# First product of the second feed-forward by Strassen's method, both of its weights converted in the first stage

## The chip, the core and the metric

The kernel runs on one NeuronCore of one Trainium2 chip. The metric is the device time of one execution in microseconds (us); the time of the kernel before is the median of three runs. The engines are TensorE (PE: matrix products, with PEld for loading the stationary operand), VectorE (DVE), ScalarE (ACT), GpSimd (POOL) and SyncE (SP), which here issues nearly all DMAs. Each engine works off its own queue in order.

## The reference

```python
scores = x @ state^T / 8;  a = softmax(scores);  xread = a @ state         # per batch and head: 512 x 64, 32 states
scores2 = state @ x^T / 8; a2 = softmax(scores2); sread = a2 @ x
x = concat(xread, sread) -> (8 * 544) x 512 tokens
x = (sigmoid(x @ w_gate) * (x @ w_val)) @ w_out                             # first feed-forward, 512 -> 1536 -> 512
r = maximum(x @ w_in, 0); out = (r * r) @ w_out2                            # second feed-forward, 512 -> 2048 -> 512
```

The weights arrive as float64. The kernel holds every operand of a product as a high and a low part in TensorE's fp32r type and forms each product of tiles with three matmuls (high by high, high by low, low by high): that is `mm3`.

## The kernel before

**Stages.** Tokens are worked in nine blocks: eight of 512 (one per batch, `b` = 0 to 7) and one of 256 with the state tokens of all batches (`b` = 8). The first stage runs 108 units, each one slice `f` of 128 of the 1536 hidden features for one block. `front_x` makes the gate and value products (12 matmuls of 512 columns), the sigmoid (ACT) and their product `g` (DVE); `split_g` splits `g` into `gh` (ACT) and `gl` (DVE); `back1` multiplies by the first `w_out` (12 matmuls) into four PSUM banks `acc0` to `acc3`. Units 0 to 95 are the token blocks; the last twelve (the state stage, `front_s`) are the state block's, with matmuls of 256 columns and weights `ws` that come back from DRAM. Attention, the conversion of the weights and the products of states and weights are laid beside the units by `spread(fns, start, end)`, which gives each step a time in units; `step()` calls what is due. A block's output is stored in `y_dram[b]`.

**The second feed-forward.** `front2(b, f)` multiplies one block by one slice of `w_in` (12 matmuls of 512 columns, four tiles of 128 along the 512 inputs by three), then relu (ACT), square (DVE) and split (ACT, DVE); `back2(b, f, g)` multiplies by a slice of the second `w_out` (12 matmuls) into the four `acc` banks, which collect all 16 slices of a block. So a token block takes 16 x 24 = 384 matmuls of 512 columns, and the state block 192 of 256 and 96 of 512.

**Weights.** `load_raw` fetches 512 KB of float64, and `convert` makes fp32r parts of it: one ScalarE instruction on the low words, five on VectorE (`q`, three `tensor_scalar` on `c`, and the addition `c<-c,q`), then the high part on ScalarE and the low part on VectorE (`busy` is False, so the helper is VectorE).

```python
        nc.scalar.copy(out=w[:, 0, :], in_=cf)
        helper(busy).tensor_sub(out=w[:, 1, :], in0=cf, in1=w[:, 0, :].bitcast(F32))
```

The second feed-forward's 32 tiles are converted by `feed()`: two in the middle of the first stage, four about the state stage, the rest beside the first blocks of the second feed-forward; then all of them stay in SBUF.

**Order.** The instructions are written in the order of the program, and a scheduler then sets each engine's queue by its own estimate of times. Waits are by semaphore: an instruction that waits holds up everything behind it on its engine. Buffers come from pools; a tile of a pool waits until the last reader of the tile whose place it takes is done.

## Time and profile before

| what | value |
|---|---|
| median of three runs | 1541.22 us (1539.25 to 1543.1) |
| the profiled execution | 1542.9 us from its first to its last instruction; its own time is not given apart |
| TensorE busy | 1491.6 us, 97% |
| VectorE, ScalarE, GpSimd busy | 854.6, 724.1, 214.7 us |
| first stage's token blocks and attention | up to about 734 us |
| state stage | about 734 to 789 us |
| second feed-forward | 789 to 1542.9 us |

Matmuls are pipelined: the duration of one (about 390 ns at 512 columns) is longer than the distance at which they follow one another, so a stretch is read by how many matmuls ran in it. The busy share is an average over stages with different limits; a stage is read in its own stretch.

### The profile page before, as it was taken

To read this page: it belongs to the slowest core of one execution; us is meant where nothing else is said; L and a number is where in the kernel's file an instruction comes from. 1 tells how busy PE (TensorE), PEld (TensorE's weight loads), DVE (VectorE), ACT (ScalarE), POOL (GpSimd) and SP (SyncE) were. 2 spreads that over 40 slices of the span, in tenths; PEclk is the share of its full clock that TensorE was granted. 3 is DMA by queue.
4 is the path that set the end of the run, shared out by engine and by line. 5 is a ranking of instruction groups with operands and counts; after the bars stand their busy time and mean duration, and the time that the engine had idled before them with its cause. 6 is when DMAs were issued, how large, how long until landed. Compare 5 with 4: busy or idle time off the path is not lost.

```text
span 1542.9 us, 19143 instructions
## 1 busy us (share of the span) xinstructions
PE 1491.6 (97%) x6744; PEld 1193.9 (77%) x6744; DVE 854.6 (55%) x1550; ACT 724.1 (47%) x1314; POOL 214.7 (14%) x263
## 2 busy tenths in 40 slices
PE   5889999999998999999999999999999999999998
PEld 3558767777776778888898788888888888888887
DVE  7987887778986755555659823323232323323232
ACT  5676765456676867665335522223232222223222
POOL 1123213222332333433000000000000000000000
PEclk8789999999999999999999999999999999999999
DMA  9783888879976433343925300101010000101000
GB/s 280 231 225 97 216 272 284 279 234 256 283 208 172 139 94 110 89 116 108 382 91 152 108 28 4 52 0 55 1 55 0 28 28 0 55 0 42 1 28 15
DMA packets 173105, 185.82 MB, mean 120 GB/s; under 512 B 99536, under 2 KB 108752, under 8 KB 171984
## 3 DMA queue, kind: packets, MB, share of 16 engines
q1 hardware_dynamic: 170736, 183.81, 38.9%
q8 instruction: 53, 0.87, 0.2%
q10 hardware_dynamic: 2272, 0.79, 0.2%
q14 instruction: 44, 0.36, 0.1%
HBM read 120.59 MB, written 63.96 MB: 120 GB/s over the span
## 4 chain that ended last, share of the span: by engine, by line
PE 88%; DVE 6%; DMA 3%; ACT 2%; issue 1%; SPq 0%; DVEq 0%; ACTq 0%
PE acc L192 13%; PE acc L193 13%; PE acc L194 13%; PE psi L194 8%; PE psi L192 8%; PE psi L193 8%; PE ps_g L475 3%; PE psg L192 3%; PE psv L192 3%; PE psg L193 3%; PE psg L194 3%; PE psv L194 3%; PE psv L193 3%; DMA raw<-in_moe_w_out_dram 1%; DMA raw<-in_moe_w_val_dram 1%
## 5 line engine op out<-in xcount | busy, mean ns | idle before, releaser
L200 DVE TENSOR_TENSOR gl<-g,gh 128x512 fp32r<-128x512 f32 (+1 forms) x252 | 179.8, 713 | 235.0 <-ACT gh L199 222.2
L199 ACT CAST gh<-g 128x512 fp32r<-128x512 f32 (+1 forms) x252 | 150.5, 597 | 242.4 <-PE acc L193 212.7
L726 DVE TENSOR_TENSOR g<-r 128x512 f32<-128x512 f32 (+1 forms) x144 | 95.2, 661 | 233.5 <-ACT r L725 233.2
L192 PE MATMUL psi<-xh,wi 128*128 128x512 f32 (+1 forms) x576 | 217.7, 378 | 2.1 <-ACT wi L149 2.1
L194 PE MATMUL psi<-xh,wi 128*128 128x512 f32 (+1 forms) x576 | 217.2, 377 | 0.3 <-DVE wi L150 0.3
L193 PE MATMUL psi<-xl,wi 128*128 128x512 f32 (+1 forms) x576 | 217.3, 377 | 0.0
L192 PE MATMUL acc<-wu,gh 128*128 128x512 f32 x544 | 212.1, 390 | 0.8 <-ACT gh L199 0.8
L193 PE MATMUL acc<-wu,gh 128*128 128x512 f32 x544 | 211.9, 389 | 0.0
L542 POOL TENSOR_TENSOR gg<-gi,gg 128x256 fp32r<-128x256 f32 x192 | 156.4, 833 | 397.1 <-ACT gg L541 396.9
L725 ACT ACTIVATE r<-psi 128x512 f32<-128x512 f32 (+1 forms) x144 | 82.5, 573 | 274.1 <-PE psi L194 274.1
L194 PE MATMUL acc<-wu,gl 128*128 128x512 f32 x544 | 206.3, 389 | 0.0
L193 PE MATMUL acc<-gl,o 128*128 128x512 f32 (+1 forms) x432 | 164.0, 382 | 0.1
L194 PE MATMUL acc<-gh,o 128*128 128x512 f32 (+1 forms) x432 | 162.6, 379 | 0.0
L192 PE MATMUL acc<-gh,o 128*128 128x512 f32 (+1 forms) x432 | 141.9, 384 | 1.4 <-ACT gh L199 1.4
L192 PEld LDWEIGHTS psi<-xh,wi 128*128 128x128 f32 x576 | 108.3, 188 | 24.2 <-ACT wi L149 3.7
L194 PEld LDWEIGHTS psi<-xh,wi 128*128 128x128 f32 x576 | 108.2, 188 | 20.6 <-DVE wi L150 0.7
L193 PEld LDWEIGHTS psi<-xl,wi 128*128 128x128 f32 x576 | 108.4, 188 | 20.3
L192 PEld LDWEIGHTS acc<-wu,gh 128*128 128x128 f32 x544 | 102.1, 188 | 22.4 <-ACT gh L199 1.7
L194 PEld LDWEIGHTS acc<-wu,gl 128*128 128x128 f32 x544 | 102.2, 188 | 21.3
L193 PEld LDWEIGHTS acc<-wu,gh 128*128 128x128 f32 x544 | 102.2, 188 | 20.5
L193 PEld LDWEIGHTS acc<-gl,o 128*128 128x128 f32 x432 | 81.4, 188 | 19.2 <-issue 2.9
L192 PEld LDWEIGHTS acc<-gh,o 128*128 128x128 f32 x432 | 79.0, 189 | 20.6 <-issue 2.4
(122 smaller groups left out, 2422.5 us busy)
## 6 DMA issues: line engine op xcount, KB each, us to landing
gd<-go SPq DMA_DIRECT2D x192, 128.0 KB, 3.4
gi<-gd SPq DMA_DIRECT2D x96, 256.0 KB, 3.6
raw<-in_moe_w_out_dram SPq DMA_DIRECT2D x28, 512.0 KB, 4.4
raw<-in_moe_w_gate_dram SPq DMA_DIRECT2D x48, 256.0 KB, 4.4
raw<-in_moe_w_val_dram SPq DMA_DIRECT2D x48, 256.0 KB, 4.5
wd<-w SPq DMA_DIRECT2D x24, 512.0 KB, 4.1
ws<-wd SPq DMA_DIRECT2D x24, 512.0 KB, 9.5
xn<-in_x_dram SPq DMA_DIRECT2D x32, 256.0 KB, 3.7
```

The lines of the kernel that those rows point to most:

```text
L192: nc.tensor.matmul(ps, lh, rh, start=start, stop=False)
L193: nc.tensor.matmul(ps, lh, rl, start=False, stop=False)
L194: nc.tensor.matmul(ps, ll, rh, start=False, stop=stop)
L199: nc.scalar.copy(out=gh[:, :n], in_=g32[:, :n])
L200: nc.vector.tensor_sub(out=gl[:, :n], in0=g32[:, :n], in1=gh[:, :n].bitcast(F32))
L475: nc.tensor.matmul(ps[j], st_t[rows, l, m, c, :], w[rows, r, :], start=(i == 0), stop=(i == 2))
L542: nc.gpsimd.tensor_sub(out=t[:, 1, g], in0=src, in1=t[:, 0, g].bitcast(F32))
L725: nc.scalar.activation(out=r[:, :n], in_=ps[:, :n], func=AF.Relu)
L726: nc.vector.tensor_mul(out=g32[:, :n], in0=r[:, :n], in1=r[:, :n])
```

## The change

The second feed-forward takes the token blocks in four pairs (`p`) and the hidden features in eight pairs of slices (`q`). For one pair of blocks and one pair of slices the product with `w_in` is a 2 by 2 block product (A11 to A22 of the weights by slice and half of the 512 inputs, B11 to B22 of the tokens by half and block). Before it takes eight block products; now Winograd's form of Strassen's method takes seven, P1 to P7, each of 2 x 3 matmuls of 512 columns. Its sums of weights (S1 to S4) are made once; its sums of tokens (T1 to T4, `x_steps`) once for each pair of blocks, and the seven operands are split into high and low parts (14 tiles each, one copy on ScalarE and one subtraction on VectorE). `front` accumulates P1, P6, P7, P4 in the bank `px`, P5 and P3 in `pz`, P2 in `py`, copies three intermediate states out with ScalarE (`p1`, `p5`, `u`), and joins them to the others with three additions on VectorE; then come square and split of four results. `back` sums two slices in PSUM and adds the result to `y2` in SBUF with VectorE (ScalarE copies the first).

All 32 weight tiles are now converted in the first stage (`prep_steps`, spread from unit 57.2 to unit 94) with sums and two of the low parts on GpSimd; the parts are stored in DRAM (`wi_dram`, `wo_dram`) and read back as needed, 256 KB for each product (`wi`, twelve buffers) and 512 KB for each slice of `w_out` (`wo`, four buffers). The state block is worked in the last pair, by the plain method. The ring of `ws` tiles has eight places instead of ten.

```diff
+    NQ = NF2 // 2
+    wi_dram = {q: dram.tile([P, 8, 2, 256], F32, name=f"wi{q}") for q in range(NQ)}
+    wo_dram = {f: dram.tile([P, 2, 512], F32, name=f"wo{f}") for f in range(NF2)}
...
+        two["prep"] = gen2.enter_context(
+            tc.tile_pool(name="prep", bufs=1, side="right", reuse_waits="tile")
+        )
...
+        jobs = []
+        for q in range(NQ):
+            jobs += [("i", 2 * q), ("i", 2 * q + 1), ("u", 2 * q), ("u", 2 * q + 1)]
...
+        def single(n):
+            cs[n] = to_single(raws.pop(n), False).rearrange("p (s x) -> p s x", s=2)
+
+        def store_u(n):
+            w = two["prep"].tile([P, 2, 512], F32R, tag="w", name="wu")
+            cf = cs.pop(n).rearrange("p s x -> p (s x)")
+            nc.scalar.copy(out=w[:, 0, :], in_=cf)
+            nc.gpsimd.tensor_sub(out=w[:, 1, :], in0=cf, in1=w[:, 0, :].bitcast(F32))
+            nc.sync.dma_start(out=wo_dram[jobs[n][1]], in_=w.bitcast(F32))
+
+        def add(n):
+            a1, a2 = cs[n], cs[n + 1]
+            t = two["prep"].tile([P, 4, 256], F32, tag="s", name="sums")
+            nc.gpsimd.tensor_add(out=t[:, 0], in0=a2[:, 0], in1=a2[:, 1])
+            nc.gpsimd.tensor_sub(out=t[:, 1], in0=t[:, 0], in1=a1[:, 0])
+            nc.gpsimd.tensor_sub(out=t[:, 2], in0=a1[:, 0], in1=a2[:, 0])
+            nc.gpsimd.tensor_sub(out=t[:, 3], in0=a1[:, 1], in1=t[:, 1])
+            sums[n] = t
+
+        def blocks_of(n):
+            w = two["prep"].tile([P, 4, 2, 256], F32R, tag="hl", name="wa")
+            for c, at in ((cs.pop(n), slice(1, 3)), (cs.pop(n + 1), slice(0, 4, 3))):
+                nc.scalar.copy(out=w[:, at, 0], in_=c)
+                nc.vector.tensor_sub(out=w[:, at, 1], in0=c, in1=w[:, at, 0].bitcast(F32))
+            nc.sync.dma_start(out=wi_dram[jobs[n][1] // 2][:, 0:4], in_=w.bitcast(F32))
+
+        def sums_of(n):
+            w = two["prep"].tile([P, 4, 2, 256], F32R, tag="hl", name="ws")
+            t = sums.pop(n)
+            nc.scalar.copy(out=w[:, :, 0], in_=t)
+            nc.vector.tensor_sub(out=w[:, :, 1], in0=t, in1=w[:, :, 0].bitcast(F32))
+            nc.sync.dma_start(out=wi_dram[jobs[n][1] // 2][:, 4:8], in_=w.bitcast(F32))
+
+        steps += [lambda: load(0), lambda: load(1)]
+        for n in range(len(jobs)):
+            steps.append(lambda n=n: single(n))
+            if n + 2 < len(jobs):
+                steps.append(lambda n=n: load(n + 2))
+            if n % 4 == 1:
+                steps += [lambda n=n: add(n - 1), lambda n=n: blocks_of(n - 1), lambda n=n: sums_of(n - 1)]
+            elif n % 4 > 1:
+                steps.append(lambda n=n: store_u(n))
+        return steps
 
...
-            tc.tile_pool(name="gv2", bufs=10, side="right", reuse_waits="tile")
+            tc.tile_pool(name="gv2", bufs=8, side="right", reuse_waits="tile")
...
+    A21, A11, A12, A22, S1, S2, S3, S4 = range(8)
+    PRODUCTS = [("P1", A11), ("P5", S1), ("P6", S2), ("P2", A12), ("P7", S3), ("P3", S4), ("P4", A22)]
...
+        for name, bufs in (("wi", 12), ("wo", 4), ("g2", 18), ("y2", 10), ("t2", 1)):
...
+    def load_wo(q):
+        for f in (2 * q, 2 * q + 1):
+            t = two["wo"].tile([P, 2, 512], F32R, tag="wo", name="wo")
+            nc.sync.dma_start(out=t.bitcast(F32), in_=wo_dram[f])
+            wo[f] = t
+    def load_xin(p, i):
+        half, b = ((0, 0), (0, 1), (1, 1), (1, 0))[i]
+        t = raw_p.tile([P, 2, S], F32, tag="raw", name="xin")
+        nc.sync.dma_start(out=t, in_=y_dram[2 * p + b][:, 2 * half : 2 * half + 2, :])
+        xin[p, half, b] = t
+    def split_x(p, name, k, src):
+        h = two["x"].tile([P, S], F32R, tag="x", name="xh")
+        l = two["x"].tile([P, S], F32R, tag="x", name="xl")
+        nc.scalar.copy(out=h, in_=src)
+        nc.vector.tensor_sub(out=l, in0=src, in1=h.bitcast(F32))
+        xop[p, name, k] = (h, l)
+    def x_steps(p):
+        t1, t2 = {}, {}
+        def one_two(k):
+            b11, b12, b22 = (xin[p, i, j][:, k, :] for i, j in ((0, 0), (0, 1), (1, 1)))
+            split_x(p, "P1", k, b11)
+            t1[k] = cv_p.tile([P, S], F32, tag="c", name="t1")
+            nc.vector.tensor_sub(out=t1[k], in0=b12, in1=b11)
+            split_x(p, "P5", k, t1[k])
+            t2[k] = q_p.tile([P, S], F32, tag="q", name="t2")
+            nc.vector.tensor_sub(out=t2[k], in0=b22, in1=t1.pop(k))
+            split_x(p, "P6", k, t2[k])
+        def rest(k):
+            b12, b22, b21 = (xin[p, i, j][:, k, :] for i, j in ((0, 1), (1, 1), (1, 0)))
+            split_x(p, "P2", k, b21)
+            t3 = cv_p.tile([P, S], F32, tag="c", name="t3")
+            nc.vector.tensor_sub(out=t3, in0=b22, in1=b12)
+            split_x(p, "P7", k, t3)
+            split_x(p, "P3", k, b22)
+            t4 = cv_p.tile([P, S], F32, tag="c", name="t4")
+            nc.vector.tensor_sub(out=t4, in0=b21, in1=t2.pop(k))
+            split_x(p, "P4", k, t4)
+        return [
+            lambda: one_two(0), lambda: one_two(1), lambda: load_xin(p, 3),
+            lambda: rest(0), lambda: rest(1),
+        ]
+    def product(ps, p, q, name, start):
+        w = take_wi((p, q, name, dict(PRODUCTS)[name]))
+        for k in range(2):
+            h, l = xop[p, name, k]
+            mm3(
+                ps, w[:, 0, k, :], w[:, 1, k, :], h, l,
+                start and k == 0, k == 1, not start,
+            )
+    def snap(ps, name):
+        t = two["t2"].tile([P, S], F32, tag=name, name=name)
+        nc.scalar.copy(out=t, in_=ps)
+        return t
+    def squared(key, c, raw=False):
+        if raw:
+            r = g_p.tile([P, S], F32, tag="sg", name="r")
+            nc.scalar.activation(out=r, in_=c, func=AF.Relu)
+            nc.vector.tensor_mul(out=r, in0=r, in1=r)
+            c = r
+        else:
+            nc.vector.scalar_tensor_tensor(
+                out=c, in0=c, scalar=0.0, in1=c, op0=ALU.max, op1=ALU.mult
+            )
+        h = two["g2"].tile([P, S], F32R, tag="g2", name="g2h")
+        l = two["g2"].tile([P, S], F32R, tag="g2", name="g2l")
+        nc.scalar.copy(out=h, in_=c)
+        nc.vector.tensor_sub(out=l, in0=c, in1=h.bitcast(F32))
+        g2[key] = (h, l)
+    def front(p, q):
+        x = mm_p.tile([P, S], F32, tag="mm", name="px")
+        y = at_p.tile([P, S], F32, tag="at", name="py")
+        z = at_p.tile([P, S], F32, tag="at", name="pz")
+        def joined(ps, t):
+            c = g_p.tile([P, S], F32, tag="g32", name="c")
+            nc.vector.tensor_add(out=c, in0=ps, in1=t)
+            return c
+        product(x, p, q, "P1", True)
+        p1 = snap(x, "p1")
+        product(z, p, q, "P5", True)
+        p5 = snap(z, "p5")
+        product(x, p, q, "P6", False)
+        u = snap(x, "u")
+        product(y, p, q, "P2", True)
+        squared((p, 0, 2 * q), joined(y, p1))
+        product(x, p, q, "P7", False)
+        c22 = joined(x, p5)
+        product(z, p, q, "P3", False)
+        squared((p, 1, 2 * q + 1), c22)
+        product(x, p, q, "P4", False)
+        squared((p, 1, 2 * q), joined(z, u))
+        squared((p, 0, 2 * q + 1), x, raw=True)
+    def back(p, b, q, nt):
         for t in range(nt):
             ts = slice(t * P, (t + 1) * P)
+            acc = acc_p.tile([P, S], F32, tag=f"acc{t}", name=f"o{t}")
+            for i in range(2):
+                f = 2 * q + i
+                gh, gl = g2[p, b, f]
+                mm3(acc, gh[:, ts], gl[:, ts], wo[f][:, 0, :], wo[f][:, 1, :], i == 0, i == 1)
+            if q == 0:
+                y = y2[b, t] = two["y2"].tile([P, DM], F32, tag="y2", name="y2")
+                nc.scalar.copy(out=y, in_=acc)
+                continue
+            y = y2[b, t]
+            nc.vector.tensor_add(out=y, in0=acc, in1=y)
+            if q < NQ - 1:
+                continue
+            if b == 2:
                 for i in range(4):
                     r0 = (4 * t + i) * (S + NS) + S
                     (nc.scalar if i % 2 else nc.sync).dma_start(
+                        out=out[r0 : r0 + NS, :], in_=y[NS * i : NS * (i + 1), :]
                     )
             else:
+                r0 = (2 * p + b) * (S + NS) + t * P
+                nc.sync.dma_start(out=out[r0 : r0 + P, :], in_=y)
...
-    def feed():
-
-        if waiting and (len(waiting) > 1 or not plan2):
-            key, raw, ring = waiting.pop(0)
...
+    spread([close_gen2], 57, 57)
+    spread(prep_steps(), 57.2, 94)
+    for i in range(3):
+        spread([lambda i=i: load_xin(0, i)], u_s + 2, u_s + 2)
...
+    load_wo(0)
+    for fn in x_steps(0):
+        fn()
+    last = NP - 1
+    for p in range(NP):
+        for q in range(NQ):
+            front(p, q)
+            if p == last and q == 0:
+                prep_state_x()
+            if p == last:
+                state_front(p, q)
+            if q == NQ - 1 and p < last:
+                for fn in x_steps(p + 1):
+                    fn()
+            if p < last and NQ - 5 < q < NQ - 1:
+                load_xin(p + 1, q - NQ + 4)
+            for r in ([q - 1] if q else []) + ([q] if q == NQ - 1 else []):
+                if (p, r) != (last, NQ - 1):
+                    load_wo((r + 1) % NQ)
+                for b in range(2):
+                    back(p, b, r, NT)
+                if p == last:
+                    back(p, 2, r, NSTATE // P)
```

**What stands in SyncE's queue where the second feed-forward begins.** `ws` are the last weights of the state stage, `yd<-y` the stores of the state block's output, which wait for its last copies out of PSUM. Before:

```order
L578 DMA ws<-wd_0_238 128x1024
L578 DMA ws<-wd_1_239 128x1024
L578 DMA ws<-wd_2_240 128x1024
L578 DMA ws<-wd_3_241 128x1024
L634 DMA yd_270<-y 128x256 x4
L118 DMA raw<-in_moe_w_out_dram 128x1024
L118 DMA raw<-in_moe_w_in_dram 128x4x256
L118 DMA raw<-in_moe_w_out_dram 128x1024
L118 DMA raw<-in_moe_w_in_dram 128x4x256
```

After:

```order
L563 DMA ws<-wd_3_241 128x1024
L619 DMA yd_294<-y 128x256 x4
L742 DMA wo<-wo_270 128x1024
L742 DMA wo<-wo_271 128x1024
L727 DMA wi<-wi_262 128x512 x7
L727 DMA wi<-wi_263 128x512 x5
L742 DMA wo<-wo_272 128x1024
L742 DMA wo<-wo_273 128x1024
L873 DMA xst<-yd_294 128x1024
```

Before, the raw weights stand behind the stores, and the first slices of the second feed-forward are converted already; now the first `wo` and all the first `wi` stand behind the stores.

**What stands in VectorE's queue between two units of the token blocks** (the products `g32` number 70 and 71 of 96). Before, from the one to the other:

```order
L564 TENSOR_TENSOR g32_6061<-psv_6054,sg_6052 128x512
L200 TENSOR_TENSOR gl_6069<-g32_6061,gh_6068 128x512
L419 TENSOR_TENSOR tmp_5847<-ps_sr_5842,tmp_5847 64x256
L420 TENSOR_TENSOR sw_5793<-tmp_5847 64x128
L386 TENSOR_TENSOR et_5904<-ps_e2_5899,et_5904 128x8x64
L366 TENSOR_REDUCE nm_6034<-e2_5992 128x1
L367 TENSOR_SCALAR nm_6034<-nm_6034 128x1
L564 TENSOR_TENSOR g32_6123<-psv_6116,sg_6111 128x512
```

After, the last twelve rows ahead of the second of these (L118 to L134 are the conversion, `ws` is the low part of the weight sums):

```order
L134 ISA c_6634<-c_6634,q_6635 128x1024
L359 RECIPROCAL sum_6005<-sum_6005 128x1
L118 TENSOR_SCALAR c_6711<-raw_6522 128x512
L130 TENSOR_SCALAR q_6791<-raw_6670 128x512
L122 TENSOR_SCALAR c_6711<-c_6711 128x512
L126 TENSOR_SCALAR c_6711<-c_6711 128x512
L134 ISA c_6711<-c_6711,q_6712 128x1024
L118 TENSOR_SCALAR c_6790<-raw_6670 128x512
L130 TENSOR_SCALAR q_6849<-raw_6749 128x512
L676 TENSOR_TENSOR ws_6610<-sums_6548,ws_6610 128x4x256
L122 TENSOR_SCALAR c_6790<-c_6790 128x512
L549 TENSOR_TENSOR g32_6331<-psv_6324,sg_6315 128x512
```

Before, six instructions stand between the two products, all of attention or of the unit; now 21 do, and 14 of them belong to the conversion.

## Rows read from the trace of the kernel before

**Rows 1.** The page's head, busy times of the engines, chain that ended last

```profile
span 1542.9 us, 19143 instructions
...
PE 1491.6 (97%) x6744; PEld 1193.9 (77%) x6744; DVE 854.6 (55%) x1550; ACT 724.1 (47%) x1314; POOL 214.7 (14%) x263
...
PE 88%; DVE 6%; DMA 3%; ACT 2%; issue 1%; SPq 0%; DVEq 0%; ACTq 0%
```

**Rows 2.** Busy us (instructions) per engine by stretch, granted clock, DMA share, GB/s

```profile
200.00:440.00 240.00, 238.28 (x977) 170.27 (x976) 199.03 (x351) 144.68 (x266) 63.27 (x80) 1.00 0.86 267
439.90:680.80 240.90, 231.44 (x1061) 188.06 (x1060) 150.72 (x285) 172.37 (x325) 90.73 (x101) 0.98 0.46 127
...
800.00:820.00 20.00, 20.00 (x90) 16.57 (x89) 19.72 (x44) 11.53 (x19) 0.00 (x0) 1.00 0.49 161
900.00:1400.00 500.00, 500.00 (x2208) 414.01 (x2207) 149.04 (x217) 131.02 (x218) 0.00 (x0) 1.00 0.06 22
```

**Rows 3.** Lines by form, TensorE, 900 to 1400 us: busy us, mean ns

```profile
L192 PE MATMUL psi<-xh,wi 128*128 128x512 f32 x368 | 143.2, 389 | 0.0
```

**Rows 4.** The page's costliest groups, TensorE: busy us, mean ns, idle before, releaser

```profile
L192 PE MATMUL psi<-xh,wi 128*128 128x512 f32 (+1 forms) x576 | 217.7, 378 | 2.1 <-ACT wi L149 2.1
```

**Rows 5.** Lines by form, VectorE, 200 to 500 us: a weight conversion's six instructions

```profile
L146 DVE CUSTOM_DVE_ANT_0 c<-c,q 128x1024 uint16<-128x1024 uint16 x33 | 24.1, 733 | 0.5
L150 DVE TENSOR_TENSOR w<-c,w 128x512 fp32r<-128x512 f32 x28 | 20.1, 717 | 2.4 <-ACT w L149 2.4
L134 DVE TENSOR_SCALAR c<-c 128x512 f32<-128x512 f32 x33 | 19.1, 582 | 0.4
L138 DVE TENSOR_SCALAR c<-c 128x512 uint32<-128x512 uint32 x33 | 17.3, 527 | 0.3
L142 DVE TENSOR_SCALAR q<-raw 128x512 uint16<-128x512 uint16 x33 | 17.1, 518 | 5.1 <-DMA raw<-in_moe_w_val_dram 4.8
L130 DVE TENSOR_SCALAR c<-raw 128x512 uint32<-128x512 uint32 x33 | 16.2, 493 | 0.3
```

**Rows 6.** Lines by form, VectorE, 500 to 720 us

```profile
L200 DVE TENSOR_TENSOR gl<-g,gh 128x512 fp32r<-128x512 f32 x36 | 34.4, 955 | 17.7 <-ACT gh L199 17.4
L564 DVE TENSOR_TENSOR g<-psv,sg 128x512 f32<-128x512 f32 x35 | 24.0, 686 | 24.2 <-ACT sg L558 10.5 <-PE psv L194 8.5 <-PE ps_so L429 4.9
```

**Rows 7.** Lines by form, VectorE, 900 to 1400 us

```profile
L200 DVE TENSOR_TENSOR gl<-g,gh 128x512 fp32r<-128x512 f32 x92 | 63.7, 692 | 157.2 <-ACT gh L199 146.6 <-PE psi L193 10.6
```

**Rows 8.** Lines of the whole span: ScalarE's and GpSimd's forms

```profile
L542 POOL TENSOR_TENSOR gg<-gi,gg 128x256 fp32r<-128x256 f32 x192 | 156.4, 833 | 397.1 <-ACT gg L541 396.9
...
L128 ACT ACTIVATE q<-raw 128x512 uint16<-128x512 uint32 x92 | 72.9, 794 | 41.7 <-DVE c L146 26.3 <-DMA raw<-in_moe_w_val_dram 6.5 <-issue 4.9
...
L149 ACT CAST w<-c 128x512 fp32r<-128x512 f32 x48 | 29.8, 620 | 16.3 <-DVE c L146 8.5 <-PE ps_g L475 5.7 <-issue 1.6
```

**Rows 9.** Timeline, TensorE, end of the state stage: start, us, instruction

```profile
789.24 0.28 PE L194 MATMUL acc<-gh,o 128*128 128x256 f32 x1
789.36 0.40 PE L192 MATMUL psi<-xh,wi 128*128 128x512 f32 x1
```

**Rows 10.** Timeline, SyncE's queue: start and us of the issues

```profile
794.49 1.78 SPq L634 DMA_DIRECT2D yd<-y  x4
```

**Rows 11.** DMA issues: count, KB each, median us to landing

```profile
gi<-gd SPq DMA_DIRECT2D x96, 256.0 KB, 3.6
...
raw<-in_moe_w_in_dram SPq DMA_DIRECT2D x16, 512.0 KB, 4.8
```

**Rows 12.** Stretches of 2 us after TensorE had stood (columns as in rows 2)

```profile
494.00:496.00 2.00, 0.87 (x4) 0.58 (x3) 0.32 (x2) 0.92 (x5) 0.34 (x1) 0.50 1.08 336
...
498.00:500.00 2.00, 2.00 (x9) 1.70 (x8) 0.87 (x2) 1.51 (x5) 0.72 (x1) 0.50 0.55 143
500.00:502.00 2.00, 2.00 (x11) 1.65 (x10) 1.47 (x3) 1.95 (x6) 0.85 (x1) 0.99 0.47 131
```

**Rows 13.** Lines of the whole span: VectorE's squaring in the second feed-forward

```profile
L726 DVE TENSOR_TENSOR g<-r 128x512 f32<-128x512 f32 (+1 forms) x144 | 95.2, 661 | 233.5 <-ACT r L725 233.2
```

More of the change, by code (lines that the diff above doesn't have):

```diff
@@ L119, in load_raw, with to_single @@
         return raw
[L121 removed]
+    def to_single(raw, busy):
         lo, hi = raw[:, :, 0], raw[:, :, 1]
@@ L148, in convert @@
         )
+        return cf
+    def convert(raw, w, busy):
+        cf = to_single(raw, busy)
         nc.scalar.copy(out=w[:, 0, :], in_=cf)
@@ L731, in back2 @@
-    def back2(b, f, g):
-        nt = width(b) // P
-        if f == 0:
-            accs[b] = new_acc()
-        acc = accs[b]
-        gh, gl = g
-        w = need(("u", f))
+        for name, bufs in (("wi", 12), ("wo", 4), ("g2", 18), ("y2", 10), ("t2", 1)):
+            two[name] = ctx.enter_context(
+                tc.tile_pool(name=name, bufs=bufs, side="right", reuse_waits="tile")
+            )
+    NP = B // 2
+    wi, wo, xin, xop, g2, y2 = {}, {}, {}, {}, {}, {}
+    wi_plan = []
+    for p in range(NP):
+        for q in range(NQ):
+            wi_plan += [(p, q, name, at) for name, at in PRODUCTS]
+            if p == NP - 1:
+                wi_plan += [(p, q, "s", at) for at in (A11, A12, A21, A22)]
@@ new lines, with feed_wi, take_wi @@
+    wi_done = [0, 0]
+    def feed_wi(n):
+        while wi_done[0] < min(wi_done[1] + n, len(wi_plan)):
+            p, q, name, at = key = wi_plan[wi_done[0]]
+            t = two["wi"].tile([P, 2, 2, P], F32R, tag="wi", name="wi")
+            nc.sync.dma_start(
+                out=t.bitcast(F32), in_=wi_dram[q][:, at].rearrange("p l (k f) -> p l k f", k=2)
+            )
+            wi[key] = t
+            wi_done[0] += 1
+    def take_wi(key):
+        feed_wi(11)
+        assert wi_plan[wi_done[1]] == key
+        wi_done[1] += 1
+        return wi.pop(key)
@@ L857 @@
         held.append(lambda b=b, f=f, lo=lo, hi=hi, g=g: back1(b, f, lo, hi, g))
-        if b == B and f == 2:
-            prefetch(0)
-    for _ in range(NA):
-        feed()
     drain(0)
```

159 lines of the change are left out of this document (52 added, 107 removed).

## Prediction

> **What bounds the kernel now.** I read the page's head first: of a span of 1542.9 us TensorE is busy for 97%, and the chain that ended last lies on it for 88% [rows 1]. A busy share is a mean over stages, so I next took the stretches [rows 2]. In the second feed-forward, from 900 to 1400 us, TensorE has no gap, the granted clock is 1.00, the upper of its two levels, and VectorE and ScalarE are busy for under a third of it. The reader is to see that 2208 matmuls went through in 500 us, one per 500 / 2208 = 0.2264 us; the 0.389 us that the lines give for one matmul [rows 3] is its duration with the overlap in it and would overstate any saving. Here only fewer matmuls help, or a wait that is taken away. Between 439.9 and 680.8 us, where the conversion is put, TensorE is the fullest as well (231.4 of 240.9 us), but VectorE works for 150.7, ScalarE for 172.4 and GpSimd for 90.7 [rows 2]: idle are 90.2, 68.5 and 150.2 us. That is the room the conversion has.
>
> The sum is made against the profiled execution, whose span is 1542.9 us; the median of the runs lies 1.7 us lower, and I take that off at the end.
>
> **Fewer matmuls.** For a pair of blocks and a pair of slices there are 7 products of 6 matmuls in place of 8: 4 pairs x 8 pairs of slices x 6 = 192 matmuls of 512 columns go. The products with the second `w_out` keep their number, and so does the state block. 192 x 0.2264 = **-43.5 us**. The feed of converted weights beside the first blocks goes too, and with it the waits of `psi` for the high part: **-2.1** [rows 4].
>
> **The conversion in the first stage.** On VectorE a tile takes three operations on `c`, one `q` and one addition: 0.582 + 0.527 + 0.493 + 0.518 + 0.733 = 2.853 us [rows 5]. With 32 tiles that is 91.3 us. For the low parts come 16 instructions of 0.717 [rows 5], 11.5 us, and 8 of twice that size, put at 1.43, 11.5 us: in all 184 instructions and 114.3 us. Two conversions stood in this stretch before: 2 x 3.57 = 7.1 us go. So 107 us are to go into 90 us of idle VectorE: 17 too many. The queues are in order, and a product `g` waits behind the conversion instructions that stand before it (14 of the 21 in the piece of order shown), so not every gap is filled; I add 5 for that: **+22 us**. The nearest whole stretch, 200 to 440 us, had VectorE busy for 199 of 240 us at TensorE's side with no visible delay [rows 2]; here it is to be busy all the time. The bounds: if the durations overlap as in 800 to 820 us, where 44 instructions, most of them of conversions, filled 19.72 us [rows 2], one per 0.448, the 184 take 82 us and fit: 0. TensorE's own order is unchanged in this stage, so I see no gain below that. Upward: `gl`, of the same form as the low part, took 0.692 us where GpSimd had no work [rows 7] and 0.955 in 500 to 720 us beside it [rows 6]; the low part stands at 0.717 in rows 5. If all of the 114.3 us stretched by 0.955 / 0.717 = 1.33, it would be 152, and less 7 and 90, 55 too many. I stay at 22, since the rows of 5 come from a stretch that has GpSimd's work beside it too.
>
> That same comparison is where a rule speaks against this change. The Trainium skill (SBUF — State Buffer, Who interferes with whom) says that VectorE's second pair of ports is shared with GpSimd under an exclusive lock, so that of two such instructions one waits out the other. By that rule `gl`, with two inputs in SBUF, should stretch and `g`, with one in PSUM, should not, and the trace agrees: `g` stays at 0.686 us beside GpSimd [rows 6], `gl` does not. By the rule alone the stage would cost the upper bound, which is the third rival's.
>
> ScalarE gets 32 x 0.794 for `q` [rows 8], 32 high parts of 0.620 [rows 8] and eight of double size among them more, about 50 us of its 68.5; GpSimd 32 sums of 128x256 at 0.833 [rows 8] and 16 low parts of twice the size at about 1.67: 53 us of its 150. Both fit, though ScalarE barely, and each high part stands between two VectorE instructions. The DMAs grow most: 30 more raw tiles, 16 parts of `w_out` of 512 KB and 16 of `w_in` sums and blocks of 1 MB are about 40 MB in this stretch, beside the 31 that its mean of 127 GB/s makes: some 295 GB/s. From 200 to 440 us, with as many conversions, 267 GB/s filled 0.86 of the DMA engines and TensorE worked on [rows 2], so I count no time of its own; but loads land later, and SyncE's queue holds all of them in order behind stores that wait for low parts. That is part of what the upper bound stands for.
>
> **The state stage.** Loads of `xin` stand among the `ws` loads in SyncE's queue, splits of tokens stand in VectorE's and ScalarE's ahead of state products, and `ws` has eight places in place of ten. A load of 512 KB lands in 4.8 us [rows 11]. One such landing exposed, or a bit more, is the upper bound, 8 us; the lower is 0; I take **+3**, half of one landing and a little.
>
> **Where the second feed-forward begins.** Before, `psi` follows the last `acc` shown within 0.12 us [rows 9], and other products of the state stage are laid beside it. After, the first `wo` and `wi` stand in SyncE's queue behind four stores of `yd`, and these wait for the state stage's last copies out of PSUM (0.6 us by the nearest copy [rows 8]). So TensorE waits for the copy, four issues of 1.78 us together [rows 10], the issues of two `wo` (0.45 each, by the same row), a landing of 3.6 us for 256 KB [rows 11] and part of the 1 MB of `wo` ahead: about 7.3 us. After standing, the clock is 0.50, the lower level, and is at 0.99 only in the third stretch of 2 us after work resumed [rows 12]; 4 to 5 us at half pace lose 2.2. **+9.5**, between 5 (the `wi` pass the `wo` on other DMA queues, and no fall of the clock) and 14 (both `wo` land whole before it).
>
> **The turns between pairs.** At each of three turns the tokens of the next pair are added and split: 14 splits and 8 sums on VectorE, together with the last results of the old pair some 40 instructions of 0.69 us or 27.6, beside the last round's 111 matmuls, 25.1 us. Short by 2.5 us at each, less if it begins earlier: between 0 and 7.5, **+5**.
>
> **The rounds between.** A round has 90 matmuls, 20.4 us. VectorE has 3 joins and eight additions into `y2`, each with one input in PSUM, as `g` has at 0.686 [rows 6], three squarings by an instruction that has no row (nearest: 0.661 [rows 13]), one more squaring, and four low parts of 0.692 [rows 7]: 19 instructions, 13 us or 64%. ScalarE has less. The waits that are new (P6 waits for the copy of P1 out of its bank, P7 for that of P6, P4 for the join) have five or more microseconds of other products between them in TensorE's order. So 0; the cover is gone if VectorE runs a few microseconds late, which is the last rival's price. Weights read back are 2.8 MB a round, 140 GB/s, below the 161 that a stretch has shown [rows 2].
>
> Sum: -43.5 - 2.1 + 22 + 3 + 9.5 + 5 = -6.1, so 1536.8, and less 1.7 **1535 us**.
>
> **The rivals.** (1) The conversion is nearly hidden: VectorE's gaps take it, as the pitch of 0.448 us allows, and the stage costs 8, the state stage 1, the start 7, the turns 0.5. -45.6 + 16.5 = -29.1: **1512 us**. For it speaks that TensorE's order in the first stage is the same and a unit has slack ahead of it; against, that ScalarE and VectorE hand each tile to and fro five times in order. (2) VectorE becomes the bound of the first stage, slowed by GpSimd, whose work rises from 90.7 to about 144 us in that stretch: the products `g`, and the loads behind the stores that wait for VectorE, come late, and TensorE waits in each unit. The stage costs 45, nearer to the bound of 55 than to the forecast's 22, and the rest is as forecast: -45.6 + 62.5 = +16.9, **1558 us**, slower. It decides from 28 us on, where the sum is zero. For it speaks 0.955 against 0.692; against, that the rows of 5 include some of that. (3) The change saves matmuls but TensorE waits in each round, for the squaring without a row, or for a join, about 1 us in each of 32 rounds: +32, **1567 us**. For it speaks only that this instruction isn't in the trace; against, 36% of VectorE's time to spare.
>
> **How the numbers follow.** The forecast has 0.42, with its own range from 1522 (stage at its middle, others low) to 1547; rival 1 has 0.26, rival 2 0.24, rival 3 0.08. No change, within 0.3% (about what a measurement of this kernel can tell), is 1536.6 to 1545.8. Faster: rival 1 and a little over half of the forecast's, 0.49. Same: 0.17. Slower: rivals 2 and 3 and a sliver, 0.34. The range runs from 1508, a little below rival 1, to 1562, a little above rival 2.
>
> **What would show it.** In the profile after: in a stretch of steady rounds as long as 900 to 1400 us about 2208 matmuls still; fewer would mean rival 3, with TensorE idle by `px` or `pz` released by VectorE or ScalarE. The last token unit of the first stage at about 734 + 22 us, with TensorE's idle time named after `gl` or `gh`; at 742 it is rival 1, at 779 rival 2, and then `w`, `wa` and `ws` take 1.2 times their 0.717 per 512 elements or more. TensorE idle for 7 us ahead of the first `px`, released by the `wi` load, and the clock at 0.50 behind it. The prediction is wrong if the matmuls of the rounds don't stand 0.2264 us apart, or if the conversion delays the first stage by something other than VectorE.

## The result, and the profile after

| | median of the runs | profiled execution's span | TensorE busy | granted clock, mean |
|---|---|---|---|---|
| before | 1542.01 us (4 runs) | 1542.9 us | 1491.6 us | 0.982 |
| changed | 1555.61 us (4 runs) | 1554.3 us | 1470.6 us | 0.971 |

The ratio is 1.0085, 95% interval 1.0071 to 1.0100: slower by 13.6 us. The forecast was 1535 and faster; the time lies inside its range of 1508 to 1562, on the side that had a chance of 0.34.

The page's head after, against [rows 1]: TensorE is busy for 21 us less and yet the span is 11 us longer, VectorE has 250 us more.

```profile
span 1554.3 us, 19917 instructions
...
PE 1470.6 (95%) x6552; PEld 1169.8 (75%) x6552; DVE 1104.3 (71%) x1897; ACT 739.8 (48%) x1343; POOL 280.5 (18%) x311
...
PE 80%; DVE 7%; DMA 4%; ACT 4%; issue 3%; POOL 2%; SPq 0%; ACTq 0%; POOLq 0%; DVEq 0%
```

To see where the time went, cut both spans at the same work: at the start of the 58th of VectorE's 108 products `g` (the conversion has begun), of the 94th (its steps end by there), of the 97th (the first of the state block) and of the 108th (the last). Counted from one like this, they belong to the units 57, 93, 96 and 107. Busy times by stretch, columns as in rows 2; before:

```profile
481.44:716.59 235.15, 225.69 (x1052) 186.12 (x1051) 131.68 (x257) 163.77 (x314) 90.11 (x99) 0.98 0.40 112
716.59:741.86 25.27, 22.20 (x114) 18.33 (x113) 19.58 (x37) 13.67 (x28) 2.76 (x3) 1.00 0.61 236
741.86:788.19 46.33, 45.97 (x380) 45.42 (x379) 17.74 (x44) 13.17 (x29) 0.00 (x0) 1.00 0.70 257
```

After, the same three stretches and 500 us of steady rounds:

```profile
481.10:763.03 281.93, 242.98 (x1040) 190.31 (x1040) 237.17 (x423) 197.38 (x372) 153.75 (x145) 0.93 0.73 233
763.03:794.15 31.12, 25.60 (x128) 21.91 (x126) 18.03 (x36) 18.45 (x35) 5.36 (x5) 0.89 0.59 203
794.15:839.62 45.47, 45.00 (x375) 45.00 (x376) 16.96 (x36) 11.29 (x27) 0.00 (x0) 1.00 0.60 221
900.00:1400.00 500.00, 500.00 (x2241) 415.46 (x2240) 316.04 (x497) 152.72 (x265) 0.00 (x0) 1.00 0.49 167
```

The conversion's stretch lasts 281.9 us in place of 235.2, 46.8 more. Subtract TensorE's busy time from the length: it stood for 39.0 us instead of 9.5, and was "busy" for 243.0 instead of 225.7 with the same matmuls. Of this second part, 17.3 us, the clock makes about 11: read in stretches of 0.5 us, TensorE was busy at the lower level, 0.50, for 30.1 us instead of 8.4, and half of that is lost. The other 6 us are busy time at the upper level that these rows don't divide further. The next stretch costs 5.9 more, the state block 0.9 less. From the last `g` to the end (788.19 to 1542.9, 839.62 to 1554.3) it is 714.7 us instead of 754.7: the second feed-forward gives back 40.0, and 51.8 - 0.3 (the 58th product began that much earlier) - 40.0 is the 11.4 by which the spans differ (rounded by 0.1).

What TensorE waited for in the conversion's stretch (total, times, longest, us):

```profile
PE psg L186 <- ACT sg L543: 20.7, 10, 6.0
PE acc L186 <- ACT gh L193: 3.2, 4, 1.5
PE ps_sr L396 <- POOL xs L385: 2.6, 2, 2.3
PE acc L187 <- DVE gl L194: 2.4, 4, 1.5
```

The sigmoid `sg` frees the bank of PSUM for a later `psg`. It came up to 6 us late, and the timeline shows what stood before it in the longest case. ScalarE, up to the longest wait (start, us, idle before it in brackets):

```profile
655.61 0.18 ACT L424 COPY xs_t<-ps_so 64x32 f32<-64x32 f32 x1 [3.09 <-DVE xs_t L426]
658.34 0.62 ACT L652 CAST wu<-c 128x512 fp32r<-128x512 f32 x1 [2.55 <-DVE c L134]
658.87 0.77 ACT L116 ACTIVATE q<-raw 128x512 uint16<-128x512 uint32 x1
659.66 1.28 ACT L357 ACT_TABLE_LOAD   x1
...
662.57 1.28 ACT L543 ACT_TABLE_LOAD   x1
663.86 0.60 ACT L543 ACTIVATE sg<-psg 128x512 f32<-128x512 f32 x1
```

VectorE in the same microseconds:

```profile
652.72 0.95 DVE L118 TENSOR_SCALAR c<-raw 128x512 uint32<-128x512 uint32 x1 [0.64 <-POOL sums L661]
653.59 1.77 DVE L194 TENSOR_TENSOR gl<-g,gh 128x512 fp32r<-128x512 f32 x1
655.40 0.18 DVE L426 COPY xs_t<-ps_so 64x32 f32<-64x32 f32 x1
655.61 0.63 DVE L122 TENSOR_SCALAR c<-c 128x512 f32<-128x512 f32 x1
656.27 0.85 DVE L126 TENSOR_SCALAR c<-c 128x512 uint32<-128x512 uint32 x1
657.16 1.11 DVE L134 CUSTOM_DVE_ANT_0 c<-c,q 128x1024 uint16<-128x1024 uint16 x1
```

And TensorE:

```profile
664.51 0.80 PE L186 MATMUL psg<-a,gg 128*128 128x512 f32 x1 [6.04 <-ACT sg L543]
```

VectorE waits for GpSimd's sums before it may write `c`; then `gl` takes 1.77 us; a copy of attention that ScalarE waits for comes after it; then ScalarE's next instruction, the high part `wu`, waits for the end of the conversion of `c`; only behind that come the exponential of attention and the sigmoid, with an `ACT_TABLE_LOAD` of 1.28 us before each. Two stretches of these microseconds (columns as in rows 2):

```profile
654.00:660.00 6.00, 4.17 (x19) 2.85 (x18) 5.83 (x9) 1.82 (x4) 4.68 (x5) 1.00 0.55 176
660.00:665.00 5.00, 0.49 (x1) 0.49 (x2) 3.62 (x11) 4.96 (x9) 2.09 (x3) 0.74 0.96 320
```

First VectorE is nearly full (5.83 of 6.00 us) and ScalarE waits for it, then ScalarE is (4.96 of 5.00) with what has gathered behind the wait.

### The profile page after: what moved, and what is told of

The parts are those of the page before. It is cut to its first block, busy times and chain, and to the rows that moved or that the text cites. A ratio compares the mean times of both kernels' runs of the same rounds, so it can differ in the third digit from the quotient of the medians.

```text
span 1554.3 us, 19917 instructions
## 1 busy us (share of the span) xinstructions
PE 1470.6 (95%) x6552; PEld 1169.8 (75%) x6552; DVE 1104.3 (71%) x1897; ACT 739.8 (48%) x1343; POOL 280.5 (18%) x311
## 4 chain that ended last, share of the span: by engine, by line
PE 80%; DVE 7%; DMA 4%; ACT 4%; issue 3%; POOL 2%; SPq 0%; ACTq 0%; POOLq 0%; DVEq 0%
PE o L187 8%; PE o L188 8%; PE o L186 8%; PE acc L187 5%; PE acc L186 5%; PE acc L188 4%; PE px L186 4%; PE px L187 4%; PE px L188 4%; PE ps_g L463 4%; PE psg L186 3%; PE psv L186 3%; PE psg L187 3%; PE psg L188 3%; PE psv L187 2%
## 5 line engine op out<-in xcount | busy, mean ns | idle before, releaser
L858 DVE TENSOR_TENSOR y<-o,y 128x512 f32<-128x512 f32 x238 | 161.9, 686 | 81.1 <-PE o L188 79.9
L187 PE MATMUL o<-wo,g2h 128*128 128x512 f32 x544 | 211.7, 389 | 0.0
L186 PE MATMUL o<-wo,g2h 128*128 128x512 f32 x544 | 211.6, 389 | 0.0
L188 PE MATMUL o<-wo,g2l 128*128 128x512 f32 x544 | 210.3, 389 | 0.0
L188 PEld LDWEIGHTS o<-wo,g2l 128*128 128x128 f32 x544 | 102.1, 188 | 21.2
L187 PEld LDWEIGHTS o<-wo,g2h 128*128 128x128 f32 x544 | 102.1, 188 | 21.1
L186 PEld LDWEIGHTS o<-wo,g2h 128*128 128x128 f32 x544 | 102.1, 188 | 20.9
L186 PE MATMUL px<-xh,wi 128*128 128x512 f32 x256 | 99.5, 392 | 7.7 <-DMA wi<-wi 7.7
L187 PE MATMUL px<-xl,wi 128*128 128x512 f32 x256 | 100.2, 391 | 0.0
L186 PEld LDWEIGHTS acc<-gh,o 128*128 128x128 f32 x432 | 80.0, 190 | 26.3 <-ACT gh L193 5.5
L188 PE MATMUL px<-xh,wi 128*128 128x512 f32 x256 | 99.2, 391 | 0.0
L194 DVE TENSOR_TENSOR gl<-g,gh 128x512 fp32r<-128x512 f32 (+1 forms) x108 | 83.8, 775 | 20.5 <-ACT gh L193 20.4
L463 PE MATMUL ps_g<-w,st_t 64*128 64x512 f32 x288 | 84.5, 475 | 11.5 <-ACT w L141 5.4
L188 PEld LDWEIGHTS acc<-gh,o 128*128 128x128 f32 x432 | 82.8, 192 | 15.5 <-issue 0.7
```

The lines of the kernel that those rows point to most:

```text
L186: nc.tensor.matmul(ps, lh, rh, start=start, stop=False, skip_group_check=more)
L187: nc.tensor.matmul(ps, lh, rl, start=False, stop=False, skip_group_check=more)
L188: nc.tensor.matmul(ps, ll, rh, start=False, stop=stop, skip_group_check=more)
L194: nc.vector.tensor_sub(out=gl[:, :n], in0=g32[:, :n], in1=gh[:, :n].bitcast(F32))
L463: nc.tensor.matmul(ps[j], st_t[rows, l, m, c, :], w[rows, r, :], start=(i == 0), stop=(i == 2))
L858: nc.vector.tensor_add(out=y, in0=acc, in1=y)
```

## Experiments

Three theories for the 46.8 us: V, VectorE is full there; D, the transfers; H, hand-offs in in-order queues. Each run's ratio is against the kernel before as timed beside it: 1544.83 us for the first four runs, 1543.84 for the next three and the first of the runs with late pairs, 1545.31 for "High parts on VectorE" and four late pairs, 1544.19 for "VectorE alone" and five late pairs.

**One pair converted** (1508.78 us, ratio 0.9772, 0.9757 to 0.9786): seven of eight pairs of slices are left out, and the steps of the one are spread up to unit 61.8 instead of 94.

```diff
-        for q in range(NQ):
+        for q in range(1):
             jobs += [("i", 2 * q), ("i", 2 * q + 1), ("u", 2 * q), ("u", 2 * q + 1)]
```

> Leaves out the conversion of seven of the eight pairs of slices (loads, arithmetic and stores); every product reads the parts of the first pair. Theories for the 46 us that the first stage lost between products 58 and 94: V, VectorE is full there and its operations are lengthened by GpSimd's; D, the added transfers (some 40 MB) hold up the loads that the units need; H, the conversion hands each tile to and fro between VectorE, ScalarE and GpSimd, and the units wait behind it in in-order queues. All three give 1505 to 1515 us here (1555.6 less seven eighths of 46 to 52). If the loss came from the other edits of that stage (the pools that close at unit 57), the time would stay above 1535.

So the conversion is what costs: its seven pairs make 47 us of the time (50 when each kernel is set against the runs of before beside it), and with a single pair the rest of the change gains 36.

**Transfers alone** (1532.22 us, 0.9928, 0.9912 to 0.9945).

```diff
+            if n > 3:
+                copy_out(n)      # the raw tile to DRAM: 2 x 512 KB for w_in, 512 KB for w_out
+                return
```

> As the run with one pair converted, but the raw tiles of all 32 are loaded, and stored again to DRAM in the bytes and the number of the parts (1 MB for each tile of w_in, 512 KB for each of w_out); the arithmetic of the other seven pairs is left out. V and H: within 8 us of the run with one pair. D: within 10 us of the changed kernel, so over 1545.

Neither: 23.4 us above one pair. With no arithmetic to hold them back the transfers come in a burst, and TensorE is slowed in it. In the first 62 us it stands for 8.2 us more than with one pair (numbers in the last section); the rest of the loss comes up to about 720 us, at DMA shares of 0.50 to 0.98. The first 62 us (columns as in rows 2; DMA share next to last):

```profile
478.00:500.00 22.00, 12.05 (x50) 8.21 (x48) 11.09 (x21) 10.52 (x19) 7.36 (x8) 0.77 0.99 259
500.00:520.00 20.00, 16.39 (x73) 12.77 (x74) 17.85 (x34) 16.02 (x31) 10.56 (x9) 1.00 1.03 386
520.00:540.00 20.00, 16.05 (x66) 12.45 (x65) 14.03 (x26) 11.38 (x21) 4.72 (x5) 0.85 1.01 325
```

**Arithmetic alone** (1552.40 us, 1.0057, 1.0039 to 1.0075).

```diff
-            cs[n] = to_single(raws.pop(n), False)...
+            cs[n] = to_single(raws.pop(n) if n < 2 else raws[2 + n % 2], False)...
+            if n < 4:      # ahead of each store and of the loads
```

> The arithmetic of all 32 tiles stays (the tiles after the fourth are made from the third and fourth raw tile again), but 28 raw loads and all stores but those of the first pair are left out; every product reads the first pair's parts. V and H: at least 30 us above the run with one pair, 1540 to 1553. D: within 10 us of the run with one pair.

43.6 us above one pair, without 28 loads and most of the stores. D falls as the cause in the changed kernel: the arithmetic alone makes nearly all of the loss, and the two costs don't add (23 + 44 against 47).

**Nothing of the conversion on GpSimd** (1564.07 us, 1.0134, 1.0118 to 1.0149).

```diff
-            nc.gpsimd.tensor_sub(out=w[:, 1, :], in0=cf, in1=w[:, 0, :].bitcast(F32))
+            nc.vector.tensor_sub(out=w[:, 1, :], in0=cf, in1=w[:, 0, :].bitcast(F32))
```

(and the four sums likewise)

> The sums of weights and the low parts of w_out on VectorE in place of GpSimd: 48 instructions more on VectorE, 16 x 0.69 + 32 x 0.36 = 22.6 us, and 54 us less on GpSimd. If VectorE's work alone counts, 15 to 23 us slower, about 1575. V with GpSimd's share in it: the shorter operations give about as much back, 1545 to 1560. H: the waits for GpSimd's results go (30 us of GpSimd's and VectorE's idle time stand against them in the trace), 1535 to 1545.

By the ratios (1.0134 against 1.0085, intervals apart) 0.5% or 7.6 us slower than the changed kernel: above H's band, a little above that of V with GpSimd's share, and well below the 1575 of VectorE's work alone. Saving the waits for GpSimd did not pay for 15 us more of VectorE's busy time.

**One VectorE operation fewer in each conversion** (1550.81 us, 1.0043, 1.0027 to 1.0060).

```diff
-            nc.vector.tensor_scalar(out=c, in0=hi, scalar1=1, scalar2=1, op0=ALU.logical_shift_left, ...)
-            nc.vector.tensor_scalar(out=cf, in0=cf, ... op0=ALU.max, op1=ALU.min)
+            nc.vector.tensor_scalar(out=cf, in0=hi.bitcast(F32), ... op0=ALU.max, op1=ALU.min)
```

> Leaves out the first of the five VectorE operations of each of the 32 conversions (the one that takes the sign off; negative weights come out wrong): 32 instructions of 0.63 us, 20 us less on VectorE, everything else in place. V (VectorE's work is what is short): 15 to 20 us below the changed kernel, about 1537. H (the gaps in the in-order queues, not the work): at most 5 us below it, 1550 to 1556. The run that put 22.6 us more on VectorE lost only some 6, which speaks for H.

Nearer H's number than V's: 6.5 us by the ratios. VectorE's busy time fell by 14.8 us (table below) and not by 20, so each microsecond brought 0.44.

**Five pairs converted** (1536.35 us, 0.9951, 0.9936 to 0.9965): `range(5)` in place of `range(NQ)`.

> Converts five of the eight pairs of slices, spread over the same units; the products of the last three pairs read the parts of the first three. VectorE then has about 66 us more than before in a stretch where it had 103 idle. V as an overflow: at most 10 us above the run with one pair, 1509 to 1519. H, a cost for each tile that is handed about: four sevenths of the 47 us between one pair and eight, about 1535.

V as an overflow of the stretch as a whole falls: VectorE was busy for 198 of 265 us, a quarter of it idle, and still the run is 28 us above one pair (28.6 against the runs of before beside each). Between one, five and eight pairs the cost is a straight line, 7 us a pair.

But the run did not thin the conversion out, as it was meant to. The conversion's last instruction on VectorE started at 633 us with five pairs and at 726 with eight, which from 481 on is 30 to 31 us a pair in both. While it ran, VectorE was nearly as full as in the changed kernel, and behind it TensorE had few gaps. Five pairs, then the changed kernel:

```profile
520.00:560.00 40.00, 35.03 (x156) 27.04 (x157) 37.92 (x67) 29.81 (x58) 25.54 (x24) 1.00 0.73 244
560.00:600.00 40.00, 32.20 (x136) 24.75 (x135) 37.71 (x68) 30.67 (x55) 21.37 (x20) 0.93 0.68 223
640.00:680.00 40.00, 37.03 (x174) 30.32 (x173) 22.39 (x43) 26.88 (x53) 17.07 (x19) 1.00 0.37 101
...
520.00:560.00 40.00, 34.63 (x147) 27.00 (x148) 38.18 (x66) 29.09 (x58) 23.13 (x23) 0.96 0.69 241
560.00:600.00 40.00, 33.20 (x144) 25.50 (x142) 37.08 (x65) 29.92 (x53) 22.47 (x21) 0.96 0.67 215
640.00:680.00 40.00, 32.18 (x138) 25.31 (x138) 32.94 (x61) 26.62 (x50) 23.59 (x24) 0.91 0.77 247
```

So a VectorE that is nearly full for as long as the conversion runs would give the same straight line, and this run does not rule it out.

**The state block's stores on ScalarE's queue** (1551.63 us, 1.0051, 1.0036 to 1.0066).

```diff
-            nc.sync.dma_start(out=to[:, e, :], in_=y[:, :n])
+            (nc.scalar if b == B else nc.sync).dma_start(out=to[:, e, :], in_=y[:, :n])
```

> The four stores of the state block's output go out on ScalarE's queue, so the first loads of wo and wi no longer stand behind them on SyncE's. If TensorE's 7.7 us there are the stores and their wait, 2 to 5 us come back: 1550 to 1554. If the loads wait for the buffers, which the last state products release, no change.

About 5 us back, 0.34%. The one wait of 7.7 us ahead of the first `px` (below) becomes three of 0.9, 2.0 and 0.9: the stores ahead of the loads were half of it, the loads' own landing the rest.

**High parts on VectorE** (1572.87 us, 1.0181, 1.0166 to 1.0196). The stall shown above suggested to take ScalarE out of the conversion.

```diff
-            nc.scalar.copy(out=w[:, 0, :], in_=cf)
+            nc.vector.tensor_copy(w[:, 0, :], cf)
```

> The high parts of the conversion (16 for w_out, 16 and 8 of double size for w_in) are made on VectorE instead of ScalarE: 40 copies, some 24 us, more on VectorE. Theory H in its sharper form, from the trace of the changed kernel around 655 to 664 us: the sigmoid stands on ScalarE behind a copy that waits for c of the conversion, and TensorE waits for the sigmoid. Without these copies ScalarE has nothing of the conversion that waits for VectorE: the 21 us of TensorE's waits for the sigmoid mostly go, and the time is 1535 to 1548. If it is VectorE's work: 6 (by the slope of the run without GpSimd) to 24 us slower, 1562 to 1580.

My sharper theory falls. TensorE's waits up to the 94th product, to be held against the list of the changed kernel:

```profile
PE psg L186 <- ACT sg L543: 11.1, 9, 2.0
PE psv L186 <- DVE g L549: 9.7, 10, 2.2
PE acc L187 <- DVE gl L194: 7.4, 10, 1.7
```

The wait for the sigmoid is halved, as expected, and waits for VectorE's own `g` and `gl` take its place; the backlog shows behind the 94th product, where the stretch up to the 97th takes 49.5 us instead of 31.1.

**VectorE alone** (1533.95 us, 0.9933, 0.9918 to 0.9948).

```diff
+            nc.vector.tensor_scalar(out=c, in0=raws[2 + n % 2][:, :, 1], ...)
+            for _ in range(4):
+                nc.vector.tensor_scalar(out=cf, in0=cf, scalar1=LOW_END, scalar2=HIGH_END, ...)
+            # and 28 tensor_sub in all; nobody reads them
```

> One pair of slices is converted as in the changed kernel; for the other 28 tiles only VectorE works, for as long as it would: five tensor_scalar instructions for each and 28 subtractions between them, without loads, stores, ScalarE or GpSimd and with results that nobody reads (all products read the first pair's parts). Occupancy (the units' own instructions stand behind the conversion's on VectorE, whatever hands it on): 30 to 45 us above the run with one pair, 1540 to 1553. Hand-offs (the waits between VectorE, ScalarE and GpSimd cost, not VectorE's time): at most 15 us above it, under 1524.

Between the two: 25.8 us above one pair (0.6 is taken off one pair's time for the runs of before beside it). So more than half of the 43.6 that the whole arithmetic costs is there when VectorE's instructions are handed to no other engine, and with less of them than meant: VectorE has 79 us more than with one pair, the whole arithmetic 102 (table below). The rest comes with the missing work, the hand-offs and the longer instructions (`c<-c,q`, 0.856 us with GpSimd's part of the conversion beside it, [rows 5] 0.733); these runs don't part the three.

The runs whose work on VectorE differs, from the 58th product to the 97th:

| run | VectorE busy, us | length, us | TensorE standing, us |
|---|---|---|---|
| before | 151.3 | 260.4 | 12.5 |
| one pair | 157.3 | 267.2 | 15.9 |
| three pairs (below) | 183.4 | 281.1 | 25.5 |
| four pairs (below) | 198.3 | 286.2 | 28.4 |
| five pairs | 213.1 | 292.5 | 33.7 |
| VectorE alone | 236.4 | 293.5 | 30.2 |
| one operation fewer | 240.4 | 309.9 | 45.3 |
| changed kernel | 255.2 | 313.1 | 44.5 |
| arithmetic alone | 259.3 | 310.3 | 44.4 |
| without GpSimd | 270.3 | 323.2 | 55.2 |
| high parts on VectorE | 280.8 | 331.2 | 65.3 |

From one pair to eight VectorE's 97.9 us more make the stretch 45.9 longer, 0.47 us for each; from one to five 25.3 for 55.8, 0.45. The run with VectorE alone lies below this line: 26.4 for 79, 0.33.

**Part of the conversion beside the second feed-forward.** There VectorE is busy for 316 of 500 us in the changed kernel's steady rounds, so the last pairs go there (with a ring of six `wi`).

```diff
-    spread(prep_steps(), 57.2, 94)
+    spread(prep_steps(0, 5), 57.2, 94)
+    late = prep_steps(5, NQ)          # a slice of it behind each front(0, q)
```

> Five pairs of slices are converted in the first stage, the last three beside the first four rounds of the second feed-forward, where VectorE has a third of its time idle and GpSimd nothing to do; the ring of wi has six places instead of twelve to make room. V: the first stage costs some 10 us, the rounds 0 to 5 more: 1515 to 1525. H: the first stage still costs about 29, 1537 to 1545.

1538.27 us (0.9962, 0.9947 to 0.9976), 2 above the run that leaves three pairs out: by the rounds they are nearly free. V's number fails and H's holds. With four late, the stores on ScalarE's queue and the next pair's tokens loaded in one round:

> Four pairs of slices converted in the first stage, four beside the first six rounds of the second feed-forward, the state block's stores on ScalarE's queue, the next pair's tokens loaded in the last round but one. By the straight line between one, five and eight pairs (6.7 us each) the first stage gives back 7 us against five pairs, the stores some 4: 1525 to 1531. If four late pairs don't fit beside the rounds (VectorE there has 7 us idle in each of 20.4), TensorE waits for wi and it is 1535 or more.

1527.48 us (0.9887, 0.9871 to 0.9904), as the line says. With five:

> As the run with four pairs late, but five are late, beside the first six rounds. By the straight line the first stage gives back another 7 us: 1520 to 1523. If VectorE's idle third of the rounds can't hold five pairs (about 60 us of it in six rounds against 115 instructions of 0.5 to 0.7 us, 58 to 80), TensorE waits for wi in the rounds 3 to 7 and the time is 1527 or more.

1521.51 us (0.9845, 0.9829 to 0.9862): some 23 us faster than the kernel before, and still converting three pairs beside the units. Its waits of TensorE for `wi` in the second feed-forward are 1.9, 1.8 and 1.7 us, all before 830 us. Behind them its trace shows no wait of TensorE, though VectorE was all but full while the late pairs were converted:

```profile
850.00:950.00 100.00, 100.00 (x443) 82.81 (x442) 97.78 (x168) 44.27 (x71) 22.03 (x20) 1.00 0.91 323
```

## Why the prediction was wrong

**The step that failed is the conversion in the first stage, +22 forecast and 46.8 measured.** The prediction had it in two parts. The first, "17 too many", was the overflow of 107 us into 90 idle ones. Between the 58th and the 94th product VectorE has 237.2 - 131.7 = 105.5 us more, and 235.2 - 131.7 = 103.5 were idle before: 2 too many. The second, "not every gap is filled; I add 5 for that", is the one that failed: VectorE still stood for 44.8 of the 281.9 us, and 2.0 + 44.8 is the 46.8. So the idle time of an engine whose every instruction stands in line between others' was counted as room that fills almost to the end. In the dose runs each microsecond of conversion put on VectorE there lengthened the stretch by nearly half of one. The sign that I had named, TensorE's idle time after `gl` or `gh`, makes 5.6 us in the list above; the sigmoid on ScalarE makes 20.7.

How full VectorE was while the conversion ran bears on it too. Cut from 480 us to about the 94th product into stretches of 5 us, it was busy for 95% or more in none of 47 before, 3 of 48 with one pair, 17 of 53 with five and 25 of 57 in the changed kernel; in these 25 TensorE stood for 20.0 of its 38.9 us. That VectorE is full for a while does not suffice, though: the run with VectorE alone had 30 of 52 and lost less; from 200 to 440 us before, 21 of 48 such stretches were as full and TensorE stood for 1.5 us in them, and in the last run's rounds from 850 to 950 us 16 of 20 were and it stood for none.

**The lower clock was left out of that term.** I priced it where the second feed-forward begins and not in the stage where it mattered more. Of the 46.8 us, 29.5 are TensorE standing; in the other 17.3 it counts as busy with the same matmuls, some 11 of them because of the lower level (the result section has the working). Three stretches of 2 us around one of the longer waits (4.0 us, up to 504.0) show it, the lower level of 0.50 lasting on after the work has resumed:

```profile
502.00:504.00 2.00, 0.00 (x0) 0.00 (x0) 1.97 (x3) 1.97 (x4) 1.67 (x2) 0.50 1.06 413
504.00:506.00 2.00, 1.98 (x5) 1.60 (x6) 1.97 (x5) 1.87 (x4) 1.15 (x1) 0.50 1.04 377
506.00:508.00 2.00, 2.00 (x8) 1.74 (x7) 1.97 (x5) 1.11 (x4) 0.00 (x0) 0.50 0.65 217
```

VectorE is full in all three (1.97 of 2.00 us). By the waiting alone the term would have been 29.5, still 7.5 above what I wrote.

**Rival 2 had the time (1558) and half the mechanism.** (The prediction once calls it the third rival's.) Its cost of 45 was right, and its sign. That GpSimd lengthens VectorE's instructions is seen too: `c<-c,q` took 0.825 us in the stage after, against 0.733 in [rows 5]; `gl` 0.951, as in [rows 6]; `g`, with an input in PSUM, 0.682. But `gl` stood at 0.946 in this stretch before as well; of the signs named for this rival, low parts of 1.2 times their 0.717, `wa` shows it (0.882) and `ws` does not (1.214 for twice the size); and taking GpSimd out of the conversion made the kernel slower. That VectorE is the bound holds at most for the time in which the conversion ran: over the whole stretch it was busy for 84%. What I held against it, that rows 5 already include GpSimd, was true and did not decide.

**The state stage, +3**: the stretch into it took 5.9 more and the state block itself 0.9 less, inside the bounds of 0 to 8.

**The start of the second feed-forward, +9.5**, was right. TensorE's last state product and the first `px`:

```profile
842.11 0.28 PE L188 MATMUL acc<-gh,o 128*128 128x256 f32 x1
850.05 0.80 PE L186 MATMUL px<-xh,wi 128*128 128x512 f32 x1 [7.66 <-DMA wi<-wi]
850.64 0.63 PE L187 MATMUL px<-xl,wi 128*128 128x512 f32 x1
...
853.58 0.40 PE L188 MATMUL pz<-xh,wi 128*128 128x512 f32 x1
853.81 0.40 PE L186 MATMUL pz<-xh,wi 128*128 128x512 f32 x1
```

7.8 us of gap, then eight matmuls some 0.43 us apart instead of 0.23, 1.6 us.

**The turns, +5, cost nothing** that can be read: in steady rounds from 900 to 1400 us, turns included, TensorE is busy for 500.0 us and the clock is 1.00, and `py` returns after 20.4 us in the mean of seven rounds (904.85 to 1047.64 us), the 90 x 0.2264 of the prediction. That 2241 matmuls are counted there and not 2208 comes from the last pair, which has the state block's narrower ones (299 from 1340 to 1400 us, before 267). Fewer matmuls at an unchanged distance: -43.5 holds. Rival 3 is out with it, and the squaring without a row costs what its neighbours do:

```profile
L810 DVE SCALAR_TENSOR_TENSOR c<-c 128x512 f32<-128x512 f32 x80 | 53.6, 685 | 0.8
```

**What is left** of the second feed-forward's -40.0 after -43.5 and +9.4 is -5.9, for which I had -2.1 (the feed's waits). I can't divide it further by these rows; TensorE stood for 3.2 us between 820 and 900 us before, beside the feed.

So 46.8 for 22 is 25 too little; the state stretch 2 more than forecast, the turns 5 less and the rest 4 less. These make up the 17.5 us between the -6.1 of the sum and the 11.4 of the spans.

Open: whether the loss comes from the conversion's instructions standing ahead of the units' in VectorE's queue, or from VectorE being nearly full while they run. Every run that left pairs out or moved them kept the rest as dense, and none thinned the conversion out inside the stage. Open too is how the half that VectorE's instructions cost by themselves divides into standing in the queue and lengthening attention's own instructions through GpSimd; and why the conversions from 200 to 440 us [rows 2], nearly as dense and with VectorE at 83%, left TensorE almost no idle time. The stretch there has other work, and no run moved attention.

## What to carry to other kernels

Idle time of an engine with an in-order queue need not be free room if another engine's next step waits on that queue. Put added work where nobody waits for that engine: here the later rounds, where VectorE took it up to 98% of its time and TensorE did not wait. Where that can't be done, don't price it by the idle time that the mean shows; in this stage it cost nearly half of its own length. Price the lower clock along with every wait of TensorE, not at the one big gap. And when a run leaves part of the work out, look in its trace where the rest ran: five pairs of eight took five eighths of the time at the same density, so the mean over the stretch said little about how full VectorE had been.

## What was not expected of the hardware

In the run with the transfers alone the DMA engines' share was about 1.0 from 478 to 540 us, and TensorE stood for 17.5 of these 62 us, against 9.3 at a share of 0.58 with one pair and 6.0 at 0.52 before; the units' own loads were the same in all three. VectorE's `tensor_scalar` on `c` took 0.42 us with GpSimd idle (800 to 820 us, before), 0.48 to 0.58 beside GpSimd at 26% (200 to 440 us) and 0.57 to 0.63 at 55% (after): an instruction with a single input can grow beside GpSimd as well, which the prediction had not counted. The Trainium skill (SBUF — State Buffer, Who interferes with whom) says that `tensor_scalar` can contend with GpSimd in a mode that uses both pairs of ports; the longer durations agree, and the trace does not name the mode. GpSimd's share alone does not set them: in the last run's rounds, 850 to 950 us, they took 0.41 with GpSimd at 22%.
